# Half-layer values, masks and readings ahead in their queues, and casts on ScalarE in a four-layer attention kernel

## The chip, the cores and the metric

The kernel runs on one core of a Trainium2 chip. A core has five engines with instruction queues of their own: TensorE (PE, matmuls; PEld is its weight load), VectorE (DVE), ScalarE (ACT), GpSimd (POOL) and SyncE (SP, which issues the DMAs here). Each engine works through its instructions in order; semaphores tie the queues together. The metric is the device time of one execution in microseconds (us); lower is better.

## The reference

Four layers alternate: a windowed one (window 256, causal), a full one without a mask, then both again with the same weights. S = 2048 positions, D = 512, 32 heads of 16.

```python
def _A_ref(x, wqkv, wo):                      # _B_ref: the same without the mask
    qkv = (x @ wqkv).reshape(B, S, 3, H, Dh).transpose(2, 0, 3, 1, 4)
    q, k, v = qkv[0], qkv[1], qkv[2]
    scores = jnp.einsum("bhqd,bhkd->bhqk", q, k) * (Dh ** -0.5)
    mask = (idx[:, None] - idx[None, :] >= 0) & (idx[:, None] - idx[None, :] < 256)
    p = _softmax(jnp.where(mask[None, None], scores, -1e9), axis=-1)
    return einsum("bhqk,bhkd->bhqd", p, v).transpose(0, 2, 1, 3).reshape(B, S, D) @ wo
x = x + _A_ref(_layernorm(x), A_wqkv, A_wo)
x = x + _B_ref(_layernorm(x), B_wqkv, B_wo)
x = x + _A_ref(_layernorm(x), A_wqkv, A_wo)
x = x + _B_ref(_layernorm(x), B_wqkv, B_wo)
```

## The kernel before, in words

**Tiling.** Positions go in four chunks c = 0 to 3 of 512 (QC), heads in eight quarters qd of four heads (the program's count of "quarters" of a chunk), or four groups t of eight heads (NHT). For a layer l, attention runs over c and, within it, over qd; in layer 3 the outer loop is over t, with two quarters qd = 2t and 2t + 1 for each of the four chunks. The text calls (t, c) in layer 3 a part t and a query chunk c. A full quarter is 16 steps, one for each 128 keys: two score tiles of 128 x 1024 (L663), two exponentials on ACT (L667), and four matmuls of the exponentials with the values (L707, called pv), which are held two steps behind the scores. A windowed quarter is three steps; there the exponentials of the edge tiles are zeroed by masks on POOL (`affine_select`, L729 and L732) before pv (L739) may use them. The values have a 17th column of ones, so that pv also gives the softmax's sum. `epilogue` (L633 to L650) transposes the sums on DVE, divides, transposes back, splits the result into two float16 parts (head and remainder, hl), and copies them to the tiles oh by four DMAs.

**Matrices as pairs.** Weights and normed inputs are split into two float16 parts, and a product is made of three matmul terms (TERMS). A projection of a chunk (`project` for queries Q and keys K, `values` for VV, `wo` for the output OO) is therefore 48 matmuls of 512 columns, 12 for each of four PSUM banks. `project` reads a bank twice (L490 or L492 to sp, L493 the remainder), squares it (L496, L498), sums the squares by a matmul (L515) and, for keys, takes a maximum on DVE (L530, km), from which `key_shift` builds rows in the key buffer kf. Keys and queries go through DRAM (kf, kw, qs) and come back in the layout of the scores (kt, qt). `wo` adds its product to x: dx (L601), the addition (L602), then the statistics of the next layer's norm (L428, L429); behind the fourth tile of 128 rows, `norm` computes one inverse root for all four (`rsqrt`, L44 to L50, twelve tiny operations), and for each tile xn, xh and the remainder (L439, L442). A DMA transposes each xh into xc (L461). In layer 3 `wo_part` (L621, L622) does the output by groups of heads.

**Weight preparation.** PR works on a weight matrix during layer 0: loads it, takes maxima over columns on DVE (L287, two reductions), scales (L293 to L325; wd is a scale spread over columns by a matmul of ones and copied by ACT), then `parts`: for each of four slices a multiply (L333), a cast (L337) and a subtraction (L338), all on POOL. The raw weights, their parts and the full layers' values share four buffers (tag "vf").

**What sets the order.** PE's order is written by the program itself: a planner with a clock in it (MM = 0.222 a matmul) puts side work (K, Q, VV, OO, PR, transposes T) between attention steps, from a list for each chunk (`side0`, `side1`, `side2`, `side3`) in a `Side` object; what is left over is forced by `Side.finish()` in one piece, in layer 3 behind every (t, c), in layer 1 at its end. Between a windowed layer and the next full one, a tail of work stands without attention (`tails`, `lasts`). In full layers side work has one PSUM bank (acc[1]) and its matmuls are split into four quarter-column pieces each (L408). On the other engines a tile scheduler sets the order by priority: the program's order, unless a piece stands in `tc.high_priority(HEAD_START)`, which moves it ahead by 100.

## Time and profile before

| | us |
|---|---|
| median of 3 runs (lowest, highest) | 2864.93 (2863.16, 2867.7) |
| the profiled execution | 2864.46 |
| its span in the profile | 2862.7 |
| PE busy | 2668.1 (93%) |
| ACT busy | 2352.5 (82%) |
| DVE busy | 1048.1 (37%) |
| POOL busy | 627.5 (22%) |

The span starts with a prologue (to about 65 us), and then come layer 0, its tail, layer 1, layer 2, its tail, layer 3 and some 24 us of end. "Busy" counts an engine's own instructions. A row of the waits names the waiting engine, the tile and line, what it waited for, and the total in us, the count and the longest. A row of a table by stage gives the stretch, its length, and for each engine its busy time and number of instructions, then the granted clock of PE as a share of full speed, the share of the DMA engines and the GB/s moved. A row of a group of instructions gives line, engine, operation, tiles and shapes, the count, the busy total and the mean in ns of one, and the idle time before them. A row of the chain or of a timeline gives start, length, engine, line, and how many.

### The profile page before, as it was taken

How to read it: one execution, taken by the hardware profiler on the slowest of the kernel's cores; microseconds unless marked ns; L12 is line 12 of the kernel's file. 1: busy time of each engine (PE TensorE's matmuls, PEld its weight loads, DVE VectorE, ACT ScalarE, POOL GpSimd, SP SyncE). 2: the span in 40 equal slices, each digit the busy share in tenths (PEclk: the TensorE clock that was granted, in tenths of full speed). 3: DMA queues.
4: the chain of work that ended last, by engine and by line, in shares of the span. 5: the costliest groups of instructions: out<-in, count | busy, mean ns of one | idle time of the engine just before them, and what ended most of it. 6: DMA issues, size and time to landing. Idle time of an engine off the chain costs nothing.

```text
span 2862.7 us, 58733 instructions
## 1 busy us (share of the span) xinstructions
PE 2668.1 (93%) x23298; PEld 766.6 (27%) x23298; DVE 1048.1 (37%) x2194; ACT 2352.5 (82%) x2643; POOL 627.5 (22%) x1183
## 2 busy tenths in 40 slices
PE   8777989799999999999999888999999999999997
PEld 4222433322222222222223333322222222222221
DVE  7667656411113212311224667722222322223222
ACT  3443656299999999999996666569999999999996
POOL 3547565101100000000003567500000000000000
PEclk9888999899999999999999999999999999999998
DMA  6857666522223222322343665542433333333331
GB/s 225 229 181 191 219 189 201 179 101 88 88 70 104 90 70 88 111 83 70 97 112 116 177 189 146 161 135 89 126 102 103 113 121 119 111 101 110 112 97 57
DMA packets 317423, 363.10 MB, mean 127 GB/s; under 512 B 120913, under 2 KB 223825, under 8 KB 309841
## 3 DMA queue, kind: packets, MB, share of 16 engines
q1 hardware_dynamic: 317136, 359.24, 41.5%
q8 instruction: 185, 3.03, 0.4%
q14 instruction: 102, 0.83, 0.1%
HBM read 229.64 MB, written 96.99 MB: 114 GB/s over the span
## 4 chain that ended last, share of the span: by engine, by line
PE 68%; ACT 10%; DVE 8%; issue 6%; DMA 3%; POOL 3%; SPq 1%; ACTq 0%; DVEq 0%; POOLq 0%
PE acc L707 28%; PE s L663 18%; ACT e L667 9%; PE b L411 9%; PE acc L408 8%; PE acc L739 3%; PE bs L411 2%; DVE ot L633 1%; DMA oh<-hl 1%; DVE xh L442 1%; SPq L650 1%; POOL w L338 1%; POOL e L732 1%; DVE xn L439 1%; DVE xh L439 1%
## 5 line engine op out<-in xcount | busy, mean ns | idle before, releaser
L667 ACT ACTIVATE e<-s 128x1024 f32<-128x1024 f32 (+2 forms) x2432 | 2235.3, 1199 | 115.1 <-PE s L663 108.1
L707 PE MATMUL acc<-e,vt 128*17 128x512 f32 x8192 | 1078.0, 598 | 3.7 <-DVE ot L633 1.5
L663 PE MATMUL s<-qt,kt 64*128 64x512 f16 (+3 forms) x5504 | 791.1, 355 | 70.8 <-ACT e L667 36.3
L663 PEld LDWEIGHTS <-kt 64*128 64x128 f16 x5504 | 222.6, 94 | 894.6 <-issue 851.3
L646 POOL TENSOR_TENSOR hl<-o,hl 128x512 f16<-128x512 f32 x64 | 74.2, 1159 | 999.8 <-DVE hl L645 923.3
L633 DVE STREAM_TRANSPOSE ot<-acc 128x512 f32<-128x512 f32 x128 | 91.2, 712 | 545.6 <-PE acc L707 448.0
L732 POOL TENSOR_SCALAR_AFFINE_SELECT e<-e 128x256 f32<-128x256 f32 x512 | 229.6, 456 | 160.1 <-ACT e L667 159.7
L739 PE MATMUL acc<-e,vt 128*17 128x384 f32 (+2 forms) x2816 | 213.4, 398 | 27.5 <-POOL e L729 26.6
L729 POOL TENSOR_SCALAR_AFFINE_SELECT e<-e 128x256 f32<-128x256 f32 x448 | 205.3, 464 | 113.7 <-ACT e L667 111.8
L707 PEld LDWEIGHTS acc<-e,vt 128*17 128x17 f32 x8192 | 136.3, 95 | 343.6 <-issue 314.5
L411 PE MATMUL b<-xc,w 128*128 128x512 f16 x636 | 154.6, 396 | 7.3 <-DMA xc<-xh 6.2
L492 DVE TENSOR_SCALAR sp<-acc,es 128x512 f16<-128x512 f32 x32 | 23.9, 748 | 323.6 <-PE acc L408 323.6
L490 ACT ACTIVATE sp<-b,es 128x512 f16<-128x512 f32 x53 | 36.4, 687 | 123.4 <-PE b L411 119.5
L498 POOL TENSOR_TENSOR sq_h<-sp_h 128x512 bf16<-128x512 f16 x27 | 29.1, 1077 | 451.5 <-DVE sp_h L492 451.5
L408 PE MATMUL acc<-xc,w 128*32 128x512 f16 x1536 | 127.2, 379 | 0.4 <-DVE sp L493 0.2
L498 POOL TENSOR_TENSOR sq<-sp 128x512 bf16<-128x512 f16 x32 | 33.3, 1039 | 405.3 <-DVE sp L492 405.3
L411 PE MATMUL b<-wv,xc 128*128 128x512 f16 x456 | 110.1, 395 | 11.0 <-DMA wv<-wd 11.0
L408 PE MATMUL acc<-xc,w_h 128*32 128x512 f16 x1296 | 114.5, 379 | 2.3 <-DVE km L530 2.3
L586 ACT ACTIVATE vt<-b 128x512 f32<-128x512 f32 x38 | 22.7, 597 | 102.7 <-PE b L411 102.7
L621 DVE TENSOR_TENSOR dx<-acc,gcol 128x512 f32<-128x512 f32 x60 | 41.5, 691 | 178.8 <-PE acc L408 178.8
L408 PE MATMUL acc<-wo,oh 128*32 128x512 f16 x1296 | 102.8, 379 | 0.7 <-DVE m L542 0.7
L411 PE MATMUL b<-wo,oh 128*128 128x512 f16 x390 | 91.5, 384 | 9.7 <-DMA oh<-hl 9.0
(164 smaller groups left out, 1728.0 us busy)
## 6 DMA issues: line engine op xcount, KB each, us to landing
kt<-kf SPq DMA_DIRECT2D x128, 512.0 KB
qt<-qs SPq DMA_DIRECT2D x128, 256.0 KB
xd<-x SPq DMA_DIRECT2D x96, 256.0 KB
x<-xd SPq DMA_DIRECT2D x96, 256.0 KB
w<-wd SPq DMA_DIRECT2D x22, 1024.0 KB
kt<-kw SPq DMA_DIRECT2D x64, 256.0 KB
oh<-hl SPq DMA_DIRECT2D x512, 32.0 KB
wv<-wd SPq DMA_DIRECT2D x15, 1024.0 KB
```

Of the source, the lines that this page charges most:

```text
L408: nc.tensor.matmul(ps[g:g + 32], a[:, g:g + 32], b, start=(i == 0), stop=(i == len(pairs) - 1), skip_group_check=True)
L411: nc.tensor.matmul(ps, a, b, start=(i == 0), stop=(i == len(pairs) - 1))
L439: norm1 = lambda o: nc.vector.tensor_scalar(o, xs[i], mv[:, i, 0:1], y[:, i:i + 1], op0=ALU.subtract, op1=ALU.mult)
L498: nc.gpsimd.tensor_tensor(sq, sp[:, 0], sp[:, 0], ALU.mult)
L633: nc.vector.transpose(ot.rearrange("p b r -> p (b r)"), a)
L646: (nc.gpsimd if l % 2 else nc.vector).tensor_tensor(hl[:, 1], o, hl[:, 0], ALU.subtract)
L663: nc.tensor.matmul(ps[:, h, s0:s0 + wd_], kt[R * h:R * h + R, pr, kc:kc + P], qt[R * h:R * h + R, pr, qc:qc + wd_], start=True, stop=True)
L667: nc.scalar.activation(e[:, :, w0:w1], ps[:, :, w0:w1], AF.Exp, scale=SCALE)
L707: nc.tensor.matmul(a[32 * h:32 * h + DH + 1, :], V[l, j // 4][:, j % 4, 4 * qd + h, :], es_[h // 2][:, h % 2, :], start=(j == 0), stop=(j ...
L729: nc.gpsimd.affine_select(v, v, pattern=[[0, 2], [-1, P]], compare_op=ALU.is_gt, fill=0.0, base=0, channel_multiplier=1)
L732: nc.gpsimd.affine_select(v, v, pattern=[[0, 2], [1, P]], compare_op=ALU.is_ge, fill=0.0, base=0, channel_multiplier=-1)
L739: nc.tensor.matmul(a[32 * h:32 * h + DH + 1, q * P:(q + nb) * P], V[l, (4 * c + j) // 4][:, j % 4, 4 * qd + h, :], es_[h // 2][:, h % 2, s ...
```

## The change

- **Values by halves of the heads.** `values` gets `halves`. In full layers a value tile holds eight 128-key tiles of half of the heads. For layer 1 the chunks 0, 1 and 3, for layer 3 the chunks 0, 2 and 3 have only the lower half (heads 0 to 15) computed ahead of the layer; the upper halves are side work within it: in layer 1 over the first four quarters of chunk 0 (a `Side` of 64 steps with a `finish()` ahead of quarter 4), in layer 3 at (t, c) = (0, 0), (0, 2) and (1, 0). VV(1, 2) and VV(3, 1) stay whole. A half is 48 matmuls of 256 columns.
- **Moved side work.** K(1, 0) goes from the list of layer 0's chunk 1 to chunk 2, K(1, 1) from chunk 2 to 3; Q(1, 1) from layer 1 to the tail of layer 0, behind OO(0, 3); VV(3, 0) from layer 2's chunk 2 to 3.
- **Norms by tiles in the tails.** With `tail`, `wo` calls `norm` and the transpose for each tile of 128 rows, so that there are four chains of twelve tiny operations.
- **Precedence.** Masks, both readings of a projection (sp), the maximum km and dx of `wo` get the head start; the epilogue's transposition loses it in windowed layers.
- **Weight preparation.** The casts of `parts` go to ACT (L332); the maxima over columns come as four reductions of 128 columns in place of two of 256.
- **End.** The last group's dx tiles use another tag, two of its four additions go to POOL, and the last epilogue's subtraction from POOL to DVE.

```diff
@@ -282,8 +280,8 @@
-        for h in range(2):
-            f = slice(h * D // 2, (h + 1) * D // 2)
+        for h in range(4):
+            f = slice(h * P, (h + 1) * P)
@@ -331,10 +329,7 @@
-            if act:
-                nc.scalar.activation(w[:, k, 0, :], r, AF.Copy)
-            else:
-                nc.gpsimd.tensor_copy(w[:, k, 0, :], r)
+            nc.scalar.activation(w[:, k, 0, :], r, AF.Copy)
@@ -428,15 +423,16 @@
-    def norm(l, c, xs):
-        mv = ST.pop((l, c))[1]
-        y = rsqrt(nc, vp, f"{l}_{c}", mv[:, :, 1])
+    def norm(l, c, xs, tiles=range(4)):
+        mv = ST[l, c][1]
+        i0, i1 = tiles[0], tiles[-1] + 1
+        y = rsqrt(nc, vp, f"{l}_{c}_{i0}", mv[:, i0:i1, 1])
...
-        for i in range(4):
+        for i in tiles:
...
-            norm1 = lambda o: nc.vector.tensor_scalar(o, xs[i], mv[:, i, 0:1], y[:, i:i + 1], op0=ALU.subtract, op1=ALU.mult)
+            norm1 = lambda o: nc.vector.tensor_scalar(o, xs[i], mv[:, i, 0:1], y[:, i - i0:i - i0 + 1], op0=ALU.subtract, op1=ALU.mult)
@@ -486,11 +486,12 @@
-            if act:
-                nc.scalar.activation(sp[:, 0], ps, AF.Copy, scale=e)
-            else:
-                nc.vector.tensor_scalar(sp[:, 0], ps, e, None, op0=ALU.mult)
-            nc.vector.scalar_tensor_tensor(sp[:, 1], ps, e, sp[:, 0], op0=ALU.mult, op1=ALU.subtract)
+            with tc.high_priority(HEAD_START):
+                if act:
+                    nc.scalar.activation(sp[:, 0], ps, AF.Copy, scale=e)
+                else:
+                    nc.vector.tensor_scalar(sp[:, 0], ps, e, None, op0=ALU.mult)
+                nc.vector.scalar_tensor_tensor(sp[:, 1], ps, e, sp[:, 0], op0=ALU.mult, op1=ALU.subtract)
@@ -527,7 +528,8 @@
-            nc.vector.tensor_reduce(KM[l][r, c:c + 1], ph[r], axis=AX.X, op=ALU.max)
+            with tc.high_priority(HEAD_START):
+                nc.vector.tensor_reduce(KM[l][r, c:c + 1], ph[r], axis=AX.X, op=ALU.max)
@@ -564,31 +566,45 @@
-    def values(l, c, act, first=None):
-        n = f"{l}_{c}"
+    def values(l, c, act, first=None, halves=(0, 1)):
+        n = f"{l}_{c}_{halves[0]}"
+        HH, D0, D1 = H // 2, halves[0] * D // 2, (halves[-1] + 1) * D // 2
...
-            w = weights(l % 2, 2, f"v{n}")
+            w = weights(l % 2, 2, f"v{n}", D0, D1)
...
-        vt = V[l, c] = wp.tile([P, 4, H, DH + 1], F32, name=f"vt{n}",
-                               tag="vf" if l % 2 else "vw", bufs=NQ if l % 2 else VB)
-        nc.gpsimd.memset(vt[:, :, :, DH:], 1.0)
+        dst = {}
+        if l % 2:
+            for h in halves:
+                m = l, h, c // 2
+                if m not in V:
+                    V[m] = wp.tile([P, 8, HH, DH + 1], F32, name=f"vt{l}_{h}_{c // 2}", tag="vf", bufs=NQ)
+                    nc.gpsimd.memset(V[m][:, :, :, DH:], 1.0)
+                dst[h] = V[m][:, 4 * (c % 2):4 * (c % 2) + 4]
+        else:
+            vt = V[l, c] = wp.tile([P, 4, H, DH + 1], F32, name=f"vt{n}", tag="vw", bufs=VB)
+            nc.gpsimd.memset(vt[:, :, :, DH:], 1.0)
+        us = MM * (D1 - D0) / D
...
-            ps = bank()
+            ps = bank()[:, :D1 - D0]
...
-                yield from mms(ps, [(xc[:, b, k, i * P:(i + 1) * P], w[:, k, a, :]) for k in range(NC) for a, b in TERMS])
+                yield from mms(ps, [(xc[:, b, k, i * P:(i + 1) * P], w[:, k, a, :D1 - D0]) for k in range(NC) for a, b in TERMS], us=us)
...
-            if first:
-                nc.vector.tensor_tensor(vt[:, i, :, :DH], src, first[2].rearrange("p (h d) -> p h d", d=DH), ALU.mult)
-            elif act:
-                nc.scalar.activation(vt[:, i, :, :DH], src, AF.Copy)
-            else:
-                nc.vector.tensor_copy(vt[:, i, :, :DH], src)
-            yield -MM if PH["full"] else -12 * MM
-    def wo(l, c):
+            for x, h in enumerate(halves if l % 2 else (None,)):
+                to = vt[:, i, :, :DH] if h is None else dst[h][:, i, :, :DH]
+                fr = src if h is None else src[:, x * HH:(x + 1) * HH]
+                if first:
+                    nc.vector.tensor_tensor(to, fr, first[2].rearrange("p (h d) -> p h d", d=DH), ALU.mult)
+                elif act:
+                    nc.scalar.activation(to, fr, AF.Copy)
+                else:
+                    nc.vector.tensor_copy(to, fr)
+            yield -us if PH["full"] else -12 * us
+    def wo(l, c, tail):
@@ -598,11 +614,14 @@
-            nc.vector.tensor_tensor(d, ps, gcol[l % 2], ALU.mult)
+            with tc.high_priority(HEAD_START):
+                nc.vector.tensor_tensor(d, ps, gcol[l % 2], ALU.mult)
...
-            if i == 3:
+            if tail:
+                transposed(l + 1, c, i, norm(l + 1, c, xs, (i,))[0])
+            elif i == 3:
@@ -616,10 +635,11 @@
-            d = vp.tile([P, D], F32, name=f"dx3_{c}_{t}_{i}", tag="xn", bufs=1)
+            last = (c, t) == (NQ - 1, NHT - 1)
+            d = vp.tile([P, D], F32, name=f"dx3_{c}_{t}_{i}", **(dict(tag="oe") if last else dict(tag="xn", bufs=1)))
...
-            nc.vector.tensor_add(xs[i], xs[i], d)
+            (nc.gpsimd if last and i % 2 == 0 else nc.vector).tensor_tensor(xs[i], xs[i], d, ALU.add)
@@ -629,7 +649,7 @@
-        with tc.high_priority(HEAD_START):
+        with tc.high_priority(HEAD_START if l % 2 else 0):
@@ -643,7 +663,7 @@
-        (nc.gpsimd if l % 2 else nc.vector).tensor_tensor(hl[:, 1], o, hl[:, 0], ALU.subtract)
+        (nc.gpsimd if l % 2 and (l, c, qd) != (3, NQ - 1, NQD - 1) else nc.vector).tensor_tensor(hl[:, 1], o, hl[:, 0], ALU.subtract)
@@ -725,12 +745,13 @@
+                    with tc.high_priority(HEAD_START):
...
@@ -913,6 +934,9 @@
+                    if (l, c, qd) == (1, 0, NQD // 2):
+                        sd.finish()
+                        sd = Side(NT * NQD * NQ - NT * NQD // 2, works[1], works[2])
@@ -1040,10 +1064,10 @@
-            return [F((kw[3], True), (qs[0, 3], False)), K(0, 2), NN(3), T(0, 3), OO(0, 0), Q(0, 2), PR(1, 0), VV(0, 2), PR(1, 2), T(1, 0), K(1, 0)]
+            return [F((kw[3], True), (qs[0, 3], False)), K(0, 2), NN(3), T(0, 3), OO(0, 0), Q(0, 2), PR(1, 0), VV(0, 2), PR(1, 2), T(1, 0)]
...
-            return [F(*[(kf, True, k, k + 1) for k in range(NQ)]), K(0, 3), OO(0, 1), Q(0, 3), PR(1, 3), VV(0, 3), T(1, 1), K(1, 1)]
-        return [F(*[(qs[1, k], False) for k in range(NQ)]), VV(1, 0), OO(0, 2), VV(1, 1), T(1, 2), K(1, 2), Q(1, 0)]
+            return [F(*[(kf, True, k, k + 1) for k in range(NQ)]), K(0, 3), OO(0, 1), Q(0, 3), PR(1, 3), VV(0, 3), K(1, 0), T(1, 1)]
+        return [F(*[(qs[1, k], False) for k in range(NQ)]), K(1, 1), OO(0, 2), VV(1, 0, True, (0,)), VV(1, 1, True, (0,)), T(1, 2), K(1, 2), Q(1, 0)]
@@ -1051,11 +1075,15 @@
-            return [OO(2, 1), VV(2, 3), VV(3, 0), T(3, 1), K3(1, 0, True)]
-        return [OO(2, 2), T(3, 2), K3(2, 0, True)]
+            return [OO(2, 1), VV(2, 3), T(3, 1), K3(1, 0, True)]
+        return [OO(2, 2), VV(3, 0, True, (0,)), T(3, 2), K3(2, 0, True)]
+    def upper(l, c):
+        return VV(l, c, False, (1,))
...
-        a = [Q(1, c, False) for c in (1, 2, 3)]
+        a = [Q(1, c, False) for c in (2, 3)]
@@ -1068,16 +1096,19 @@
+        v = {(0, 0): 0, (0, 2): 2, (1, 0): 3}.get((t, c))
+        if v is not None:
+            a.append(upper(3, v))
...
-    works = [[side0(c) for c in range(NQ)], [side1()], [side2(c) for c in range(NQ)],
+    works = [[side0(c) for c in range(NQ)], [[upper(1, c) for c in (0, 1, 3)], side1()], [side2(c) for c in range(NQ)],
...
-    tails = {0: [OO(0, 3), VV(1, 2), T(1, 3), K(1, 3)],
-             2: [OO(2, 3), VV(3, 1), VV(3, 2), Q3(0, 0, True), T(3, 3), K3(3, 0, True)]}
-    lasts = {0: [VV(1, 3)], 2: [VV(3, 3)]}
+    tails = {0: [VV(1, 2), OO(0, 3, True), Q(1, 1, True, [("N", 1, 3)]), T(1, 3), K(1, 3)],
+             2: [VV(3, 1), OO(2, 3, True), VV(3, 2, True, (0,)), Q3(0, 0, True, [("N", 3, 3)]), T(3, 3), K3(3, 0, True)]}
+    lasts = {0: [VV(1, 3, True, (0,))], 2: [VV(3, 3, True, (0,))]}
...
-            attention(l, works[l] + [tails[l][1:]])
+            attention(l, works[l] + [tails[l]])
```

**Layer 0, quarter 4 of chunk 0.** Tiles e and s are exponentials and scores, named by chunk, quarter, step and pair; w and wr are the parts and the raw weights, wd the scale; sp and sq are a projection's readings and squares, vt values. POOL before:

```order
L337 CAST w_3_1203<-wr_3_584 128x512 x2
L338 TENSOR_TENSOR w_3_1203<-wr_3_584,w_3_1203 128x512 x2
L333 TENSOR_TENSOR wr_3_584<-wr_3_584,wd_3_1160 128x512 x2
L337 CAST w_3_1203<-wr_3_584 128x512 x2
L338 TENSOR_TENSOR w_3_1203<-wr_3_584,w_3_1203 128x512 x2
L732 AFFINE_SELECT e_0_4_2_0_1232<-e_0_4_2_0_1232 128x2x128
```

and now:

```order
L331 TENSOR_TENSOR wr_1_585<-wr_1_585,wd_1_1156 128x512
L333 TENSOR_TENSOR w_1_1196<-wr_1_585,w_1_1196 128x512 x3
L331 TENSOR_TENSOR wr_1_585<-wr_1_585,wd_1_1156 128x512
L333 TENSOR_TENSOR w_1_1196<-wr_1_585,w_1_1196 128x512
L753 AFFINE_SELECT e_0_4_2_0_1225<-e_0_4_2_0_1225 128x2x128
L750 AFFINE_SELECT e_0_4_2_0_1225<-e_0_4_2_0_1225 128x2x128
```

Ahead of the masks of step 2 stand parts of one matrix (of another than before), without casts. ACT at the same place before:

```order
L667 ACTIVATE e_0_4_1_1_1175<-s_0_4_1_1_1172 128x2x256
L490 ACTIVATE sp_0_1_3_1220<-b_1207,es 128x512
L667 ACTIVATE e_0_4_2_0_1232<-s_0_4_2_0_1227 128x1024
L496 ACTIVATE sq_0_1_3_1223<-sp_0_1_3_1220 128x512
L667 ACTIVATE e_0_4_2_1_1242<-s_0_4_2_1_1237 128x1024
```

and now:

```order
L687 ACTIVATE e_0_4_1_1_1168<-s_0_4_1_1_1165 128x2x256
L332 ACTIVATE w_1_1196<-wr_1_585 128x512 x4
L491 ACTIVATE sp_0_1_3_1213<-b_1200,es 128x512
L687 ACTIVATE e_0_4_2_0_1225<-s_0_4_2_0_1220 128x1024
L497 ACTIVATE sq_0_1_3_1216<-sp_0_1_3_1213 128x512
L687 ACTIVATE e_0_4_2_1_1235<-s_0_4_2_1_1230 128x1024
```

The four casts of a matrix (w_1) have come in ahead of a reading and of step 2's exponentials; so it is with w_3 one quarter later.

**Tail of layer 0, DVE.** x_15 is the fourth tile of chunk 3, dx its product; v, y and z are the inverse root's. Before:

```order
L601 TENSOR_TENSOR dx_3_3_5804<-b_5791,gcol_89 128x512
L602 TENSOR_TENSOR x_15_5672<-x_15_5672,dx_3_3_5804 128x512
L428 BN_STATS st_3_5749<-x_15_5672 128x6
L429 BN_AGGR mv_3_5750<-st_3_5749 128x2
L44 TENSOR_SCALAR v_3_5810<-mv_3_5750 128x4
L45 TENSOR_SCALAR y_3_5811<-v_3_5810 128x4
L46 TENSOR_SCALAR y_3_5811<-y_3_5811 128x4
L48 TENSOR_TENSOR z_3_5812<-y_3_5811,v_3_5810 128x4
L49 SCALAR_TENSOR_TENSOR z_3_5812<-z_3_5812,y_3_5811 128x4
```

and now:

```order
L48 SCALAR_TENSOR_TENSOR y_3_2_5851<-z_3_2_5852,y_3_2_5851 128x1
L435 TENSOR_SCALAR xn_3_2_5865<-x_14_5678,mv_3_5766,y_3_2_5851 128x512
L435 TENSOR_SCALAR xh_3_2_5866<-x_14_5678,mv_3_5766,y_3_2_5851 128x512
L494 SCALAR_TENSOR_TENSOR sp_0_1_2_5972<-b_5959,es,sp_0_1_2_5972 128x512
L438 TENSOR_TENSOR xh_3_2_5866<-xn_3_2_5865,xh_3_2_5866 128x512
L618 TENSOR_TENSOR dx_3_3_5884<-b_5871,gcol_89 128x512
L619 TENSOR_TENSOR x_15_5680<-x_15_5680,dx_3_3_5884 128x512
L494 SCALAR_TENSOR_TENSOR sp_0_1_3_5992<-bs_5979,es,sp_0_1_3_5992 128x512
L423 BN_STATS st_3_5765<-x_15_5680 128x6
L424 BN_AGGR mv_3_5766<-st_3_5765 128x2
L42 TENSOR_SCALAR v_3_3_5890<-mv_3_5766 128x1
L43 TENSOR_SCALAR y_3_3_5891<-v_3_3_5890 128x1
```

The chain of tile 2 now ends (xh) ahead of dx of tile 3, and the readings sp of Q(1, 1) stand in between.

**Layer 3, end of part 0 of query chunk 2, PE.** s are scores, kt and qt keys and queries, acc0 the sums, acc1 the bank of side work. Before:

```order
L663 LDWEIGHTS kt3_2_1_1_22630
L707 MATMUL acc0_81<-e3_2_1_13_0_23251,vt3_3_21321 17x512 x2
L707 MATMUL acc0_81<-e3_2_1_13_1_23255,vt3_3_21321 17x512 x2
L663 LDWEIGHTS kt3_3_0_0_23290
L663 MATMUL s3_3_0_0_0_23300<-qt3_3_0_23288,kt3_3_0_0_23290 128x512
```

and now:

```order
L683 LDWEIGHTS kt3_2_1_1_23389
L727 MATMUL acc0_81<-e3_2_1_13_0_24032,vt3_0_1_21764 17x512 x2
L727 MATMUL acc0_81<-e3_2_1_13_1_24036,vt3_0_1_21764 17x512 x2
L403 LDWEIGHTS xc3_2_21292
L403 MATMUL acc1_82<-wv3_2_1_23794,xc3_2_21292 32x256
```

The last row and its weight load stand 148 times, in a row, ahead of the first scores of query chunk 3. The same row of 148 stands at the end of part 1 of query chunk 0, one of 48 at the end of part 0 of chunk 0.

69 lines of the change are left out of this document (35 added, 34 removed).

## Prediction

> **What bounds the kernel now.** I read the page's first line, a table by stage, what TensorE (PE) waited for in the slow stages, and then single stretches. The cuts of the table: windowed layer 0 in four pieces, its tail, layer 1, layer 2, its tail, layer 3.
>
> ```profile
> span 2862.7 us, 58733 instructions
> ```
>
> ```profile
> core 0: us, PE busy (x) PEld busy (x) DVE busy (x) ACT busy (x) POOL busy (x), PEclk, DMA share, GB/s
> 65.00:160.00 95.00, 70.25 (x452) 24.13 (x452) 55.91 (x110) 42.24 (x63) 59.73 (x105) 0.86 0.71 206
> 160.00:270.00 110.00, 79.10 (x638) 30.64 (x636) 91.34 (x173) 49.88 (x61) 71.61 (x133) 0.87 0.67 194
> 270.00:385.00 115.00, 101.56 (x841) 40.69 (x842) 70.50 (x138) 62.19 (x77) 67.50 (x145) 0.93 0.67 209
> 385.00:520.00 135.00, 130.34 (x1123) 53.34 (x1122) 70.36 (x153) 79.64 (x98) 68.68 (x169) 0.99 0.71 212
> 520.00:581.00 61.00, 44.46 (x204) 18.73 (x201) 24.84 (x54) 10.20 (x17) 0.00 (x0) 0.86 0.51 165
> 581.00:1527.00 946.00, 934.22 (x8748) 221.44 (x8745) 203.21 (x453) 944.24 (x1024) 70.18 (x66) 1.00 0.29 88
> 1541.00:1840.00 299.00, 259.06 (x2567) 101.16 (x2566) 209.86 (x457) 189.84 (x225) 204.27 (x476) 0.99 0.59 169
> 1840.00:1896.00 56.00, 50.27 (x227) 21.44 (x223) 25.98 (x58) 9.60 (x16) 0.00 (x0) 0.97 0.64 192
> 1896.00:2839.00 943.00, 926.44 (x8185) 219.95 (x8183) 231.29 (x455) 939.62 (x1025) 64.69 (x58) 1.00 0.34 105
> ```
>
> The full layers (946 and 943 us) belong to ScalarE (ACT), whose exponentials fill them; PE is 98 to 99% busy beside them, so neither has room. In layer 0 no engine is full until 385 us, and PE's granted clock is 0.86, 0.87, 0.93. So the change can win in layer 0 and the tails and hardly in layers 1 and 3, to which it adds work.
>
> What PE waited for from 65 to 520 us, and the instruction groups concerned:
>
> ```profile
> PE acc L739 <- POOL e L729: 24.7, 10, 6.3
> PE b L411 <- DMA wv<-wd: 11.0, 2, 8.2
> PE b L515 <- DVE sp L493: 8.4, 1, 8.4
> PE b L292 <- DVE km L530: 4.6, 1, 4.6
> ```
>
> ```profile
> L729 POOL TENSOR_SCALAR_AFFINE_SELECT e<-e 128x256 f32<-128x256 f32 x224 | 101.1, 455 | 78.7 <-ACT e L667 77.6
> L338 POOL TENSOR_TENSOR w<-wr,w 128x512 f16<-128x512 f32 x23 | 28.7, 1255 | 0.2
> L333 POOL TENSOR_TENSOR wr<-wr,wd 128x512 f32<-128x512 f32 x20 | 26.2, 1323 | 4.3 <-ACT wd L325 4.2
> L337 POOL CAST w<-wr 128x512 f16<-128x512 f32 x20 | 13.6, 692 | 0.0
> L490 ACT ACTIVATE sp<-b,es 128x512 f16<-128x512 f32 x40 | 27.5, 687 | 97.2 <-PE b L411 95.5 <-DVE z L49 1.3 <-DMA kw<-sp 0.4
> L287 DVE TENSOR_REDUCE wa<-wr 128x256 f32<-128x1024 f32 x10 | 19.4, 1962 | 0.0
> ```
>
> **The change, part by part.**
>
> *Layer 0, work gone.* The upper halves of the values of chunks 0 and 1 leave it: 96 half-wide matmuls, 10.4 us of PE if half the width is half of the 2.60 us for 12 (row in the tail below). Where PE isn't last, less comes back: -7 (0 to -10.4).
>
> *Masks ahead.* PE waits 24.7 us in ten places for masks of 0.46 us that stand on POOL behind parts of 0.69 to 1.32 us. The order still has a multiply, three subtractions, a multiply and a subtraction ahead of the masks of step 2 of quarter 4 (2 x 1.32 + 4 x 1.26 = 7.7 us), and on ACT the casts stand four in a row ahead of exponentials; the fourth needs the multiply that POOL has behind three subtractions, 3 x 1.26 + 1.32 = 5.1 us in which exponentials can stand still. At two of the five matrices it is so, at the others I count 1 to 3 us. The 20 casts take 13.6 us from POOL and cost ACT some 20 x 0.69 (the like-shaped reading), hidden by ACT's idle half. I take -10, ends +5 (the casts stop more than the masks did) and -20.
>
> *Readings, maxima of keys, reduction in four.* 8.4 + 4.6 = 13.0 us are waits on DVE behind reductions of 1.96 us and norms; the reductions come in pieces of half that, the readings first: -10 (-4 to -13).
>
> *Values' weights.* Both loads behind the 11.0 us now stand ahead of the head copies on SP's queue: -10 (-5 to -11).
>
> K(1,0) and K(1,1) are done a chunk later: the same work, at nothing, with four readings less in DVE's second piece. The head transposition of windowed layers loses its precedence; it frees one of two accumulators, the other covers it: nothing, or +3 if a maximum piece and norms come before it each time PE returns.
>
> *Clock.* (1 - clock) x length is 13.3 + 14.3 + 8.1 = 35.7 us of PE in the first three pieces, in part while PE idled or another engine was last. It follows the waits, so part goes with them: -8 (0 to -15).
>
> [...]
>
> These are -45. But DVE is busy 91.3 of 110 us in the second piece, so nothing there gives more than 18.7, while the waits removed in it (8.4, 4.6, most of 8.2, half of the masks') and the clock come to some 28. I take 9 off: **-36 (-10 to -52)**.
>
> *Tail of layer 0.* Rows of the chain of waits, then of the timelines of SP and DVE:
>
> ```profile
> 537.08 2.60 PE b L411 x12
> 539.71 0.70 DVE dx L601
> 540.43 0.70 DVE x L602
> 541.16 0.70 DVE st L428
> 544.49 0.55 DVE xn L439
> 550.44 0.70 DVE xh L442
> 551.80 3.10 DMA xc<-xh
> 555.10 4.62 PE bs L411 x12
> 580.21 0.54 PE s L663 x4
> ```
>
> ```profile
> 574.36 1.60 SPq L684 DMA_DIRECT2D kt<-kf  x3
> ```
>
> ```profile
> 531.94 0.69 DVE L601 TENSOR_TENSOR dx<-bs,gcol 128x512 f32<-128x512 f32 x1 [7.92 <-PE bs L411]
> ```
>
> Now one chain of tiny root operations serves four tiles: 2.6 us from the end of the statistics (541.86) to the first norm (544.49). Then the norms take 6.65 us, 1.66 a tile. Before them, dx, addition and statistics are 2.15 us a tile. By tiles it is 2.15 + 2.6 + 1.66 = 6.4, and the last xh ends 25.7 us behind 531.94, at 557.6. In between stand four readings of Q(1,1) and a maximum, five of about 0.70 us: 561.1 against 551.1. K(1,3) therefore starts 10 us later. Q(1,1) only fills PE's wait; the last chunk's values, halved, give back little, since the keys' load (issued by 575.96, 3.1 us as the transfer above) lands at about 579, 1.2 us before the first scores: +10 - 1.2 = **+9 (+3 to +12)**.
>
> *Tail of layer 2.* PE waits only 3.7 us for the transposes; the same chain is some 7 us later there, PE's two halved values hide part: **+3 (-3 to +7)**. *Layer 2* loses half of VV(3,0), 5.2 us, of which ACT's waits leave most: **-4 (0 to -5)**.
>
> ```profile
> PE bs L411 <- DMA xc<-xh: 3.7, 1, 3.7
> PE s L663 <- ACT e L667: 23.9, 46, 1.1
> ```
>
> *Layers 1 and 3.* Rows: the forced work behind layer 1's last step, and two quarters (32 exponentials) of layer 3 with 16 and 21 side matmuls.
>
> ```profile
> 1527.65 2.77 PE L408 MATMUL acc<-wv,xc 128*32 128x512 f16 x48 [0.79 <-DVE vt L588]
> ```
>
> ```profile
> 2219.52:2248.84 29.32, 28.92 (x261) 6.77 (x260) 10.32 (x19) 29.32 (x33) 2.27 (x2) 1.00 0.47 142
> 2307.49:2337.86 30.37, 29.57 (x281) 7.16 (x277) 5.59 (x13) 29.65 (x34) 2.20 (x2) 1.00 0.26 78
> ```
>
> Layer 3 gets 3 x 48 half-wide matmuls. The order ends query chunk 2 of the first part and chunk 0 of the second with 148 quarter-column pieces at once (48 in a third place). 48 full ones take 2.77 us and a bank change 0.79; half-wide ones between 1.4 and 2.8, so 148 take 6.7 to 10.9. Up to four exponentials, 4 x 0.90, run meanwhile: ACT stands 3.1 to 7.3 us, twice. I take 4.5 each, 9, and 1.05 us for each of three fuller quarters (the two rows): **+12 (+3 to +19)**. Layer 1 gets 144 half-wide and gives 52 matmuls, some 4 us of PE in 946 that have 12 free: **+2 (0 to +6)**.
>
> *End.* Two of four additions of 0.70 leave DVE's chain for POOL, and the last subtraction goes the other way: **-2 (+1 to -2)**.
>
> Sum: -36 + 9 + 3 - 4 + 12 + 2 - 2 = -16. The profiled execution took 2864.46 us, 0.47 below the median: 2848.5, which I call 2848.
>
> **The rivals.**
>
> *Slower: ACT takes POOL's place in layer 0.* All terms but layer 0's make +20. If the casts hold exponentials at each of the five matrices for the 5.1 us worked out, 25 us replace the masks' 24.7, and with DVE the last engine in the second piece, only -7, the loads and a little clock remain, about -12: +8, 2873. It decides once layer 0 gives less than 14. For it: the four casts in a row; against it: ACT idles over half of 65 to 385 us.
>
> [...]
>
> *Larger gain.* Layer 0 gives its -52, the tails +5 and layer 3 +3, because PE gets ahead before the forced pieces: with the other terms -48, 2816. Against it: PE's 98%.
>
> *No change.* Layer 0 gives -20, as DVE bounds two pieces instead of one: 2864.
>
> **How the numbers follow.** Forecast 0.52 (its own range 2834 to 2859), slower rival 0.22, larger gain 0.12, no change 0.14. A 0.2% difference, 5.7 us, is about what a measurement of this kernel can tell. The forecast and the larger gain are faster, 0.64; the middle case splits, same 0.13; slower 0.23. The range takes in most of both sides: 2816 to 2877.
>
> **What would show it.** Right: the values' weights and DVE waits gone, mask waits near half, first exponential of layer 1 about 27 us earlier, two gaps of 3 to 7 us between exponentials of layer 3. Wrong: layer 0 ending at its old time with ACT waiting for POOL's multiplies; or layer 3 as long as now.

## The result and the profile after

The changed kernel takes 2868.76 us (median of 20 runs, 2864.26 to 2872.89), the kernel before, beside it, 2864.16 us. The ratio is 1.0014 with an interval of 1.0007 to 1.0021: no gain of 16 us, but 0.1% lost, inside the 0.2% that the prediction called no change. The profiled execution took 2868.72 us.

```profile
span 2866.7 us, 60869 instructions
```

The first exponential of a quarter is a fixed point of both programs, so its time in the two profiles tells where the difference arose (start in us):

| first exponential of | before | after | difference | change within the stage | forecast |
|---|---|---|---|---|---|
| layer 0's last quarter | 507.61 | 486.74 | -20.9 | layer 0: -20.9 | -36 |
| layer 1 | 580.74 | 568.58 | -12.2 | tail of layer 0: +8.7 | +9 |
| layer 2 | 1536.08 | 1527.33 | -8.8 | layer 1: +3.4 | +2 |
| layer 3 | 1896.09 | 1887.79 | -8.3 | layer 2 and its tail: +0.5 | -1 |
| layer 3's last quarter | 2808.67 | 2814.54 | +5.9 | layer 3: +14.2 | +12 |
| (end of the span) | 2862.7 | 2866.7 | +4.0 | end: -1.9 | -2 |

Layer 2 alone is 11.4 us shorter (forecast -4) and its tail 11.9 longer (forecast +3); both miss, and only their sum is near. The same matmuls begin ahead of the border between the two, but for the halved VV(3, 0). In this table all stages but layer 0 came within 2.2 us. Layer 0 gave 15 us less than forecast, and that turned the sign.

By stage the profile after reads as follows: layer 0, its tail, layer 1, layer 2, its tail, layer 3, the end.

```profile
65.00:499.00 434.00, 365.10 (x3050) 147.50 (x3050) 285.31 (x581) 243.76 (x320) 260.13 (x532) 0.93 0.72 213
499.00:568.50 69.50, 51.89 (x252) 24.16 (x252) 33.78 (x96) 14.70 (x28) 0.00 (x0) 0.90 0.55 165
568.50:1518.00 949.50, 938.91 (x9130) 231.91 (x9127) 198.66 (x455) 945.22 (x1024) 65.97 (x62) 1.00 0.29 88
1527.00:1820.00 293.00, 254.40 (x2552) 101.50 (x2549) 213.38 (x465) 191.72 (x228) 210.51 (x483) 0.99 0.58 171
1820.00:1887.80 67.80, 46.58 (x267) 23.88 (x265) 32.24 (x96) 9.66 (x23) 0.00 (x0) 0.85 0.55 155
1887.80:2844.00 956.20, 938.08 (x8757) 230.05 (x8755) 237.82 (x467) 941.05 (x1024) 64.41 (x58) 1.00 0.35 105
2844.00:2867.00 23.00, 6.03 (x22) 1.76 (x18) 8.32 (x21) 0.20 (x1) 2.53 (x2) 0.71 0.18 56
```

Layer 1 and layer 3 are longer with the same exponentials. In the tail of layer 2 PE is busy 46.6 of 67.8 us. What PE waited for from 65 to 520 us, now:

```profile
PE s L683 <- ACT e L687: 28.2, 25, 6.4
PE b L406 <- DMA wo<-wd: 10.5, 2, 7.9
PE s L683 <- DMA kt<-kw: 7.7, 4, 3.1
PE b L406 <- DMA xc<-xh: 6.1, 1, 6.1
PE b L516 <- DVE sp L494: 4.3, 1, 4.3
PE b L290 <- DVE sp L494: 3.2, 2, 1.9
PE b L406 <- DVE km L532: 2.6, 2, 1.7
...
PE acc L760 <- POOL e L750: 1.8, 3, 0.8
```

The waits for masks (24.7 us before, 1.8 now) and for the values' weights (11.0 us) are all but gone, and others have taken their place: 28.2 us of waits for exponentials, where there were 10.4, and loads of the output's weights and of keys. ACT's own waits suggest why its exponentials are late: the casts stand for POOL's multiplies. The run with the multiplies on VectorE, below, tests it.

```profile
ACT w L332 <- POOL wr L331: 27.0, 16, 5.7
```

In layer 3 the forced pieces are plain to see. First PE at the end of part 0 of query chunk 2, then ACT at the same place:

```profile
2063.62 1.05 PE L727 MATMUL acc<-e,vt 128*17 128x512 f32 x8
2064.49 0.29 PE L403 MATMUL acc<-wv,xc 128*32 128x256 f16 x4
2065.30 1.49 PE L403 MATMUL acc<-wv,xc 128*32 128x256 f16 x48 [0.52 <-DVE vt L604]
2067.32 1.50 PE L403 MATMUL acc<-wv,xc 128*32 128x256 f16 x48 [0.53 <-DVE vt L604]
2069.34 1.49 PE L403 MATMUL acc<-wv,xc 128*32 128x256 f16 x48 [0.53 <-DVE vt L604]
2070.77 0.60 PE L683 MATMUL s<-qt,kt 64*128 64x512 f16 x4
```

```profile
2071.26 4.71 ACT L687 ACTIVATE e<-s 128x1024 f32<-128x1024 f32 x5 [5.55 <-PE s L683]
2195.73 4.72 ACT L687 ACTIVATE e<-s 128x1024 f32<-128x1024 f32 x5 [5.55 <-PE s L683]
```

ACT, which bounds the layer (busy 941.1 of 956.2 us), stands 5.55 us at each of the two places, 11.1 of the layer's 14.2 us.

### The profile page after: what moved, and what is told of

Same layout as the page of the kernel before. It is cut to its first block, busy times and chain, and to the rows that moved or that the text cites. A ratio compares the mean times of both kernels' runs of the same rounds, so it can differ in the third digit from the quotient of the medians.

```text
span 2866.7 us, 60869 instructions
## 1 busy us (share of the span) xinstructions
PE 2662.6 (93%) x24306; PEld 792.1 (28%) x24306; DVE 1061.3 (37%) x2295; ACT 2367.7 (83%) x2679; POOL 619.0 (22%) x1160
## 4 chain that ended last, share of the span: by engine, by line
PE 65%; ACT 10%; DVE 9%; issue 7%; DMA 4%; POOL 4%; SPq 1%; ACTq 0%; DVEq 0%; POOLq 0%
PE acc L727 27%; PE s L683 17%; ACT e L687 9%; PE acc L403 9%; PE b L406 8%; PE acc L760 2%; POOL w L333 1%; PE bs L406 1%; DVE ot L653 1%; DVE xh L438 1%; SPq L670 1%; POOL wr L331 1%; POOL e L753 1%; DVE xn L435 1%; POOL e L750 1%
## 5 line engine op out<-in xcount | busy, mean ns | idle before, releaser
L753 POOL TENSOR_SCALAR_AFFINE_SELECT e<-e 128x256 f32<-128x256 f32 x512 | 236.0, 469 | 126.2 <-ACT e L687 125.3
L750 POOL TENSOR_SCALAR_AFFINE_SELECT e<-e 128x256 f32<-128x256 f32 x448 | 205.4, 464 | 114.1 <-ACT e L687 112.3
L760 PE MATMUL acc<-e,vt 128*17 128x384 f32 (+2 forms) x2816 | 207.3, 399 | 3.5 <-POOL e L750 3.2
L406 PE MATMUL b<-xc,w 128*128 128x512 f16 x672 | 164.3, 397 | 19.7 <-DMA xc<-xh 17.1
L403 PE MATMUL acc<-xc,w 128*32 128x512 f16 x1344 | 109.9, 379 | 0.2 <-DVE sp L494 0.2
L406 PEld LDWEIGHTS <-w 128*128 128x128 f16 x720 | 69.3, 102 | 127.6 <-issue 52.9
L403 PE MATMUL acc<-wo,oh 128*32 128x512 f16 x1296 | 103.3, 379 | 1.2 <-DVE m L544 0.7
L604 DVE COPY vt<-acc 128x256 f32<-128x256 f32 (+1 forms) x36 | 18.4, 512 | 230.3 <-PE acc L403 230.3
L406 PE MATMUL b<-wo,oh 128*128 128x512 f16 x390 | 92.7, 388 | 10.5 <-DMA wo<-wd 10.5
L493 DVE TENSOR_SCALAR sp_h<-acc,es 128x512 f16<-128x512 f32 x27 | 20.0, 741 | 217.6 <-PE acc L403 217.5
```

Of the source, the lines that this page charges most:

```text
L403: nc.tensor.matmul(ps[g:g + 32], a[:, g:g + 32], b, start=(i == 0), stop=(i == len(pairs) - 1), skip_group_check=True)
L406: nc.tensor.matmul(ps, a, b, start=(i == 0), stop=(i == len(pairs) - 1))
L493: nc.vector.tensor_scalar(sp[:, 0], ps, e, None, op0=ALU.mult)
L750: nc.gpsimd.affine_select(v, v, pattern=[[0, 2], [-1, P]], compare_op=ALU.is_gt, fill=0.0, base=0, channel_multiplier=1)
L753: nc.gpsimd.affine_select(v, v, pattern=[[0, 2], [1, P]], compare_op=ALU.is_ge, fill=0.0, base=0, channel_multiplier=-1)
L760: nc.tensor.matmul(a[32 * h:32 * h + DH + 1, q * P:(q + nb) * P], V[l, (4 * c + j) // 4][:, j % 4, 4 * qd + h, :], es_[h // 2][:, h % 2, s ...
```

## The experiments

Most undo one part of the change. Times are medians; ratios are to the kernel before, measured beside it. The table behind the last one has each stage of all of them. The changes of dx's and the epilogue's precedence and those of the end were not undone by themselves.

### One norm for four tiles in the tails

```diff
-    tails = {0: [VV(1, 2), OO(0, 3, True), ...
+    tails = {0: [VV(1, 2), OO(0, 3), ...
-             2: [VV(3, 1), OO(2, 3, True), ...
+             2: [VV(3, 1), OO(2, 3), ...
```

> The changed kernel, but with one norm for all four tiles in both tails, as before the change. If the chains of tiny operations for each tile are what lengthens the tails, tail 0 gets 7 to 10 us shorter and layer 2 with its tail 8 to 12, and the time is 2849 to 2854. Rival: the tails end with Q(1, 1) and with the keys' transfers, and the four chains stand beside these; then it is within 4 us of the changed kernel, 2865 to 2871.

2860.65 us, ratio 0.9988 (0.9979 to 0.9997): 8 us less than the changed kernel by the medians, 5.1 by the profiled spans. Neither side had it right: the tail of layer 0 gets 4.6 us shorter, layer 2 with its tail 3.4, and layer 0 itself 3.3 longer. Through layer 0 the two programs run the same instructions in the same order on PE, ACT, DVE and POOL, so these 3.3 us say how far two traces of one program can differ (the granted clock from 65 us to the last quarter's first exponential is 0.92 in this one, 0.93 in the changed kernel's). Some 3 us in layer 0 of a single trace are therefore no effect of an edit. The two tails together give 8.0 us, as the medians do. So the four chains are a loss, of about half the size expected. The rest of the longer tail of layer 0 (still +4.1 us against before) stays without them: PE waits 10.6 us for the transposes even so, behind Q(1, 1).

### The casts on POOL again

```diff
-            nc.scalar.activation(w[:, k, 0, :], r, AF.Copy)
+            if act:
+                nc.scalar.activation(w[:, k, 0, :], r, AF.Copy)
+            else:
+                nc.gpsimd.tensor_copy(w[:, k, 0, :], r)
```

> The changed kernel, but with the casts of the weight parts on POOL again. If the casts on ScalarE only moved the wait from masks to exponentials, TensorE's wait for exponentials from 65 to 520 us falls from 28.2 to about 10 us, its wait for masks rises from 1.8 to some 15 or 20, and the time is within 5 us of the changed kernel's. Rival: with the masks ahead, the casts on ScalarE are a loss of their own, since ScalarE stands 27 us for POOL's multiplies; then it is 10 to 18 us faster. Other rival: POOL needs the 13.6 us, and it is 8 us or more slower.

2881.42 us, ratio 1.0056 (1.0042 to 1.0070), 13 us more than the changed kernel. Layer 0 is 14.9 us longer. Its waits of PE:

```profile
PE acc L763 <- POOL e L753: 17.0, 8, 6.2
PE s L686 <- DMA kt<-kw: 13.7, 5, 4.3
PE s L686 <- ACT e L690: 9.3, 19, 1.0
PE b L409 <- DMA wo<-wd: 8.4, 2, 5.7
...
PE acc L763 <- POOL e L756: 5.8, 1, 5.8
PE b L409 <- DMA wv<-wd: 5.4, 1, 5.4
```

The waits moved as expected (masks 22.8 us, exponentials 9.3), but the time did not stay: the third reading's number, 8 us or more slower, came true. Its reason is not shown. Masks and exponentials together are waited for 32.1 us, against 30.0 in the changed kernel; more came with the loads of weights and keys, 27.5 us (13.7 + 8.4 + 5.4) against 18.2. Why these came later with the casts on POOL was not traced. With precedence for the masks, but the casts on POOL, 22.8 of the 24.7 us of their waits stay.

### Layer 3's values whole before it

```diff
-VV(3, 0, True, (0,)) ... VV(3, 2, True, (0,)) ... VV(3, 3, True, (0,))
+VV(3, 0) ... VV(3, 2) ... VV(3, 3)
-        v = {(0, 0): 0, (0, 2): 2, (1, 0): 3}.get((t, c))
+        v = None
```

> The changed kernel, but with the values of layer 3 made whole before it (none in the layer). If the forced pieces and fuller steps cost layer 3 its 14 us, and the work goes into TensorE's waits in the tail of layer 2 (13.7 and 5.5 us), layer 3 is 13 to 15 us shorter, layer 2 with its tail up to 5 us longer: 2854 to 2859. Rival: the 15.5 us of TensorE's work cost the same wherever they are: 2866 to 2871.

2854.25 us, ratio 0.9958 (0.9944 to 0.9971), 14.5 us less than the changed kernel. From the first exponential of layer 3 to that of its last quarter the difference to the kernel before is now 0.1 us (+14.2 with the halves), and layer 2 with its tail is 3.7 us longer than in the changed kernel. So PE's work cost 14 us in layer 3 and under 4 us ahead of it, mostly in a tail in which PE waits anyway (in the changed kernel up to 13.7 us for a transpose and 5.5 for keys).

### Loads of weights first on SP's queue

```diff
-            nc.sync.dma_start(w, wd[ty, s])
+            with tc.high_priority(HEAD_START):
+                nc.sync.dma_start(w, wd[ty, s])
```

(the load of a part of the columns likewise)

> The changed kernel, but with the loads of the projections' weights given precedence on SP's queue. If the place of these loads behind the head copies makes the 10.5 us that TensorE waits for the output's weights in layer 0, that wait goes and layer 0 is 7 to 12 us shorter: 2857 to 2862. Rival: what is moved behind (copies of keys, queries and heads) is then late instead, and the time stays within 3 us of the changed kernel's.

2893.79 us, ratio 1.0099 (1.0083 to 1.0114): 25 us more. PE's waits from 65 to 520 us:

```profile
PE s L684 <- ACT e L688: 28.0, 25, 6.8
PE s L684 <- DMA kt<-kw: 27.7, 7, 8.5
PE b L407 <- DMA xc<-xh: 6.0, 1, 6.0
```

The wait for the output's weights (10.5 us) went, and that for keys grew from 7.7 to 27.7 us. Layer 0 got 10.1 us longer, and the later stages another 16. So with loads of up to 1024 KB ahead of them on SP's queue, the keys' copies of 128 and 256 KB came later for PE.

### The multiplies on VectorE

```diff
-            (nc.vector if act else nc.gpsimd).tensor_tensor(r, r, dnb, ALU.mult)
+            nc.vector.tensor_tensor(r, r, dnb, ALU.mult)
```

> The changed kernel, but with the weight parts' multiplies on VectorE (POOL keeps masks and subtractions). If ScalarE's casts stand for POOL's multiplies (27.0 us), and TensorE for the exponentials behind them (28.2), ScalarE's wait falls under 8 us, TensorE's under 15, and layer 0 is 5 to 12 us shorter: 2857 to 2864. Rival: VectorE, with 26 us more in layer 0, becomes what readings and TensorE wait for, and the time is 2868 or more.

2857.33 us, ratio 0.9977 (0.9967 to 0.9987), 11 us less than the changed kernel; layer 0 is 8.9 us shorter. ACT's casts now wait for VectorE, half as long:

```profile
ACT w L332 <- DVE wr L331: 13.1, 10, 4.7
PE s L683 <- ACT e L687: 15.8, 26, 2.7
```

ACT's waits for its casts fell from 27.0 to 13.1 us and PE's for exponentials from 28.2 to 15.8. So casts that wait on ACT behind another engine did cost the exponentials time, and the 18.9 us that the multiplies take on VectorE cost less. (POOL has less to do in this run as well; the two were not told apart.)

### Precedence taken back: masks, then readings

```diff
-                    with tc.high_priority(HEAD_START):
+                    with tc.high_priority(0):
                         if far:
```

> The changed kernel, but without precedence for the masks. If the casts alone made the masks' waits go (the run with casts on POOL kept 22.8 us of them with the precedence), these stay under 6 us and the time within 4 us of the changed kernel's, 2865 to 2873. Rival: both are needed; the masks' wait comes back by 10 us or more and the time is 2878 or more.

2869.77 us, ratio 1.0020 (1.0011 to 1.0029): no different from the changed kernel (1.0014). The masks' waits are 2.2 us without their precedence. The same edit at the readings sp and the maximum km:

> The changed kernel, but without precedence for the readings of projections (sp) and the keys' maximum (km). If these bring what the casts on ScalarE alone don't (layer 0 +1 us with them alone, -21 with the whole change, -6 with all but them), layer 0 is 8 to 15 us longer and TensorE's wait for sp and km rises from 10 us to 15 or more: 2876 to 2884. Rival: the precedence does nothing, as that of the masks: 2865 to 2872.

2869.67 us, ratio 1.0017 (1.0006 to 1.0028): no different either. TensorE's waits for sp and km are 10.6 us, against 10.7 with the precedence. Neither precedence, taken back alone, changes anything that can be measured here.

### The casts on ScalarE alone, on the kernel before

```diff
-            if act:
-                nc.scalar.activation(w[:, k, 0, :], r, AF.Copy)
-            else:
-                nc.gpsimd.tensor_copy(w[:, k, 0, :], r)
+            nc.scalar.activation(w[:, k, 0, :], r, AF.Copy)
```

> The kernel before, with one part of the change: the casts of the weight parts on ScalarE. If they are worth what the run with casts on POOL shows (13 to 15 us), the masks' wait falls from 24.7 us to under 10, TensorE's wait for exponentials rises from 10.4 by 10 to 18, and the time is 2848 to 2857. Rival: the casts pay only with masks and readings ahead; then it is within 5 us of the kernel before, 2860 to 2870.

2866.86 us, ratio 1.0008 (0.9999 to 1.0017): nothing gained.

```profile
PE s L660 <- ACT e L664: 38.7, 27, 7.7
PE b L408 <- DMA wv<-wd: 14.0, 2, 12.5
PE acc L736 <- POOL e L726: 0.8, 2, 0.6
```

Masks 24.7 to 0.8 us, exponentials 10.4 to 38.7: here one wait is exchanged for the other, and layer 0 ends 1.3 us later. The precedences, which this expectation's rival blamed, change nothing on the changed kernel, as the two runs above show; beside the casts on the kernel before they were not tried.

### Layer 1's values whole before it

```diff
-VV(1, 0, True, (0,)), VV(1, 1, True, (0,)) ... VV(1, 3, True, (0,))
+VV(1, 0), VV(1, 1) ... VV(1, 3)
-[[upper(1, c) for c in (0, 1, 3)], side1()]
+[[], side1()]
```

> The changed kernel, but with the values of layer 1 made whole before it (layer 3 keeps its halves). If work taken from layer 0 shortens it, layer 0 is 7 to 11 us longer, its tail up to 3 longer (TensorE waits 2.6 us for keys there), layer 1 some 3 us shorter: 2873 to 2880. Rival: layer 0 is not bound by TensorE there, so that taking the halves out gave nothing: 2863 to 2869.

2880.84 us, ratio 1.0054 (1.0041 to 1.0068), 12 us more than the changed kernel. Layer 0 is 10.3 us longer, the 10.4 us of PE's work that its two halves hold, and its tail 3.8. Layer 1 is 0.5 us shorter, not the 3 expected: without any halves in it, it is still 3.0 us longer than before the change. So its +3.4 us are not the halves' work; where they come from was not traced. The same idea that loses in layer 3 wins in layer 1.

### Three edits together, and a fourth

One norm for four tiles, layer 3's values whole, multiplies on VectorE:

> The changed kernel with three edits together: one norm for four tiles in the tails, layer 3's values whole before it, the parts' multiplies on VectorE. If the three losses are separate, their gains add (8 + 14.5 + 11.5 from the medians, 5 + 12.7 + 11.3 from the spans): 2835 to 2842. Rival: the tail of layer 2 has room for only one of the first two, and the time is 2845 or more.

2833.78 us, ratio 0.9889 (0.9874 to 0.9904): 1.1% faster than the kernel before and 35 us faster than the changed one. The gains add (8 + 14.5 + 11.5 = 34). With chunk 3's values of layer 1 whole as well:

> The run with three edits, and the values of chunk 3 of layer 1 whole in its tail. TensorE waits 2.6 us for keys behind them there, so half of their 5.2 us are hidden, and layer 1 loses 5.2 us of side work: within 3 us of the run with three edits. If a tail's last values are free as long as keys are awaited, it is 0 to 3 us faster; if the tail is bound by them, 2 to 3 us slower.

2836.21 us, ratio 0.9894 (0.9878 to 0.9910), not to be told from the run without it. The three edits are the best version found: it beats both kernels.

### What carries layer 0's 21 us

Two reductions of 256 columns instead of four of 128, and the planner's wait behind each as before the change:

```diff
-        for h in range(4):
-            f = slice(h * P, (h + 1) * P)
+        for h in range(2):
+            f = slice(h * D // 2, (h + 1) * D // 2)
...
-            yield wait(2)
+            yield wait(4)
```

> The changed kernel, but with the maxima over columns in two reductions of 256 columns, as before the change. Of layer 0's 21 us the halves of layer 1's values carry 10, precedences nothing. If the shorter reductions carry the rest, because readings no longer stand behind 2 us, layer 0 is 6 to 11 us longer and the time 2874 to 2880. Rival: they carry nothing, within 4 us of the changed kernel.

2882.01 us, ratio 1.0066 (1.0052 to 1.0080), 13 us more; layer 0 is 10.7 us longer. But not for the reason given: PE's wait for the reading at L516 stays (4.2 us), and ACT's wait for POOL is what grew, from 27.0 to 38.1 us, and with it PE's for exponentials, from 28.2 to 39.2 us.

```profile
ACT w L332 <- POOL wr L331: 38.1, 16, 7.4
```

With the maxima in two pieces the casts stand at other steps in ACT's order, and the longest wait of one is 7.4 instead of 5.7 us. With the casts alone ACT waited as long for POOL (37.4 us). So the reduction in four, with the planner's shorter waits, goes with shorter waits of the casts; that it is the partner without which they gain nothing is an inference from these two runs, as the casts and the reduction in four were not put into the kernel before together. By which step of the order it shortens the waits was not traced either.

The keys of layer 1 a chunk earlier, as before the change:

```diff
-T(1, 0)] ... K(1, 0), T(1, 1)] ... K(1, 1), OO(0, 2),
+T(1, 0), K(1, 0)] ... T(1, 1), K(1, 1)] ... OO(0, 2),
```

> The changed kernel, but with K(1, 0) and K(1, 1) in the lists of chunks 1 and 2, as before the change. If taking K(1, 0) out of the stretch in which VectorE is busy 91 of 110 us carries what halves and precedences don't, layer 0 is 6 to 11 us longer: 2874 to 2880. Rival: it is the same work in another place: within 4 us of the changed kernel.

2869.75 us, ratio 1.0018 (1.0009 to 1.0027): the same. Layer 0 is 6.7 us longer and its tail 6.5 shorter. So some of the changed kernel's gain in layer 0 comes back as a longer tail: twelve of the matmuls that this run begins ahead of the border come behind it in the changed kernel. Last, whole values in layer 1 and casts on POOL together:

> The changed kernel with whole values in layer 1 and casts on POOL. Layer 0 against the kernel before: -21 with the whole change, -6 without the casts, -10.5 without the halves. If the two add, it is +4 without both, and the time about 2893. If they share a limit (what the casts free on POOL and DVE can be used only where TensorE has less to do, or the other way round), it is about -6, and the time about 2881 or less.

2894.35 us, ratio 1.0099 (1.0083 to 1.0114), as if the two add: layer 0 is 2.8 us longer than before, where -20.9 + 10.3 + 14.9 = +4.3.

All runs by stage, each from one trace, as the difference in us between the start of a quarter's first exponential and that of the kernel before (last column: the span):

| run | layer 0's last quarter | layer 1 | layer 2 | layer 3 | layer 3's last quarter | span |
|---|---|---|---|---|---|---|
| changed kernel | -20.9 | -12.2 | -8.8 | -8.3 | +5.9 | +4.0 |
| one norm for four tiles | -17.5 | -13.4 | -10.5 | -13.5 | +1.2 | -1.1 |
| casts on POOL | -6.0 | +2.7 | +6.2 | +6.3 | +19.9 | +17.6 |
| layer 3 whole | -21.3 | -12.8 | -11.0 | -6.8 | -6.7 | -8.7 |
| loads first | -10.8 | +3.6 | +7.4 | +17.2 | +31.4 | +30.2 |
| multiplies on VectorE | -29.8 | -21.8 | -19.8 | -18.6 | -4.7 | -7.3 |
| no precedence, masks | -22.8 | -14.3 | -12.5 | -10.7 | +3.3 | +0.8 |
| no precedence, readings | -18.1 | -9.7 | -7.8 | -6.7 | +7.6 | +4.9 |
| before, casts alone | +1.3 | +1.9 | +2.5 | +4.0 | +4.0 | +3.3 |
| layer 1 whole | -10.6 | +2.0 | +4.9 | +6.0 | +19.5 | +17.5 |
| three edits | -29.6 | -25.0 | -21.6 | -27.6 | -27.5 | -30.1 |
| four edits | -28.5 | -21.5 | -17.5 | -26.4 | -25.8 | -28.2 |
| two reductions | -10.2 | -2.3 | +1.2 | +4.8 | +18.3 | +16.1 |
| keys earlier | -14.1 | -11.9 | -9.4 | -5.6 | +8.4 | +6.3 |
| layer 1 whole, casts on POOL | +2.8 | +16.5 | +19.4 | +20.7 | +34.2 | +31.8 |

## Why the prediction was wrong

It forecast -16 us and got +4. The step that failed is the term of layer 0, -36, and in it the three waits (masks, readings, loads) that were booked as gained at -10 each. The parts can be read from the two tables of PE's waits, with their smaller rows, and from the granted clock:

| part of layer 0's term | forecast | what the profiles show |
|---|---|---|
| work gone | -7 | -10.3 (the run with layer 1's values whole) |
| masks, with the casts on ACT | -10 | -5.1: masks 24.7 to 1.8, exponentials 10.4 to 28.2 |
| readings, maxima | -10 | -4.3: waits on VectorE of 16.5 (8.4 + 4.6 + 2.4 + 1.1 in smaller ones) to 12.2 (4.3 + 3.2 + 2.6 + 2.1 in smaller ones) |
| loads | -10 | +4.4: values' and output's weights and keys 13.8 (11.0 + 0.7 + 2.1) to 18.2 (0 + 10.5 + 7.7) |
| clock, (1 - clock) x length | -8 | -7.6: 37.0 to 29.4, each added up from shorter stretches |
| taken off for VectorE | +9 | not seen |
| sum | -36 | -22.9, measured -20.9 |

The rows are not counted alike: the first is a run, and by the run with the casts on POOL the second would be -14.9. So the near sum is partly luck. A count that does not overlap is PE's own time from 65 us to the first exponential of layer 0's last quarter. Up to there both programs run the same matmuls, but for 96 that are half as wide now. Before, then after:

```profile
65.00:507.61 442.61, 370.63 (x2940) 144.41 (x2943) 281.79 (x556) 226.64 (x290) 260.17 (x533) 0.92 0.69 205
65.00:486.74 421.74, 354.62 (x2940) 143.21 (x2943) 279.12 (x566) 236.46 (x312) 252.78 (x514) 0.93 0.72 213
```

PE's busy time fell by 16.0 us, where work and clock were forecast at -15. The time in which PE stood fell from 72.0 to 67.1 us, by 4.9, where the three waits were forecast at -30, or -21 with the 9 us taken off. Waits were removed as the prediction said; others took their place.

**Values' weights** is the largest miss, 14 us. The step looked at one load's place in SP's order, saw that it was now ahead of the head copies, and costed its wait at nothing. It did not ask which load then stands behind them. It was the output's weights (7.9 us of PE's time ahead of 317.64). The wait for keys grew too, from 2.1 to 7.7 us; why was not traced. The step said where the stall went, but not what is late next. The run with all loads first exchanged the waits again: 10.5 us of one went, and 20.0 us of another came. Orders between these were not tried.

**Readings, maxima** was sized as if waits on VectorE went with the precedence. They shrank by 4.3 us, and taking the precedence back changed nothing.

**Masks ahead** was right that the masks' waits go, and had half of the gain. The fourth cast's stall, worked out as 5.1 us from the order, was 4.7 at the first matrix and at most 5.7. What failed is that the casts' cost would be hidden by ACT's idle half: the waits for exponentials rose by 17.8 us. And the precedence, under which the step stood, has no part in it: with the casts on ACT the masks' waits are 2.2 us without it, and 0.8 us on the kernel before. The casts are worth 15 us in the changed kernel and nothing on the kernel before (+1.3). That they depend on another edit, by the runs most likely on the maxima in four reductions, was foreseen nowhere.

**The cap by VectorE**, 9 us, rests on work that does not stay in place. The stretch of quarters 1 to 6 of chunk 1 went from 103.3 to 74.8 us (183.10 to 286.42 before, 180.63 to 255.41 after), but 36 matmuls of values left it, and VectorE's work in it fell from 80.3 to 62.3 us: it moves with the planner's lists. That layer 0 got 8.9 us shorter with 18.9 us of multiplies more on VectorE speaks against a cap.

The other stages came near their numbers, not all for the reason given. Layer 3 (+14.2 for +12, two stalls of 5.55 us for 4.5 each) and the end (-1.9 for -2) fit. The tail of layer 0 (+8.7 for +9) fits by its sum: 4.6 hang on the norms by tiles, and with the keys a chunk earlier the tail is 6.5 shorter, where the prediction put their move at nothing. Layer 1 (+3.4 for +2) is luck, since +3.0 of it stays without the halves. Layer 2 and its tail (+0.5 for -1) are luck as well: -11.4 and +11.9 stand for -4 and +3.

Of the rivals, the slower one named ACT in POOL's place, and PE's waits for exponentials do show it, yet it is not what decided: with the casts back on POOL it gets slower still. "No change" was the outcome, at layer 0's -20 that it assumed; its reason, VectorE bounding two pieces, is not what the runs show. The range held the time; the forecast of a gain did not.

The clock's term, -8, stands near this trace's -7.6. After the change, too, the granted clock is low where PE stands, 0.84 from 310 to 332 us with PE busy 14.4 of 22 us, and 1.00 from 398 to 499 us with PE busy 95.7 of 101. But the run with one norm, with the same order in layer 0, has the clock of before there (0.92; over the whole execution 0.976 where the changed kernel has 0.979), so these two traces do not settle how much of the term is the change's.

## What to carry to other kernels

When a stall goes away because a transfer is issued earlier, look for the transfer that is now behind it before the gain is booked; here, with the DMA engines busy 0.72 of layer 0, the wait for the values' weights went from 11.0 us to nothing and that for the output's rose from 0.7 to 10.5. Before work is moved into a stage, see whether its bounding engine has room: the same halving of the values won 10 us where it came out of a stage bound by TensorE's work and waits (layer 0, PE busy 365.1 of 434 us), and lost 14 us in a layer whose exponentials fill their engine (ACT busy 941.1 of 956.2 us), 11.1 of it where it was forced between them. And an engine with idle time was no free place for operations that wait for a busy one: ACT, busy 243.8 of 434 us, spent 14.4 us on its casts and stood 27.0 us before 16 of them, and PE's waits for exponentials rose from 10.4 to 28.2 us. Price the wait of the queue behind such operations, not the operation.
